# Weight conversion in a fused top-k attention and two-layer MoE kernel: first-layer conversions ordered first, the low bits formed on GpSimd, one joining step on VectorE, no zero matmuls

## The chip, the cores and the metric

The kernel runs on one core of a Trainium2 chip. The metric is the device time of one execution in microseconds (us), as the median of several runs. Five engines work in it, each with a queue that it works through in order: TensorE (PE; PEld are its weight loads), VectorE (DVE), ScalarE (ACT), GpSimd (POOL) and SyncE (SP), which here issues all DMAs.

## What is computed

Attention over 4 batches of 8 heads, 576 tokens and head dimension 64, in which each query keeps only its 32 largest scores; then two pairs of dense layers over all 2304 tokens.

```python
scores = scale * np.matmul(q, k.transpose(0, 1, 3, 2))
kth = np.partition(scores, -top_k, axis=-1)[..., -top_k:-top_k + 1]      # top_k = 32
scores = np.where(scores >= kth, scores, -1000000000.0)
scores = scores - np.max(scores, axis=-1, keepdims=True)
attn = np.exp(scores)
attn = attn / (np.sum(attn, axis=-1, keepdims=True) + 1e-09)
x = np.matmul(attn, v)          # to (2304, 512)
h = np.maximum(x @ w_in, 0.0)                                   # 512 -> 2048
x = h * h @ w_out                                               # 2048 -> 512
h = np.maximum(np.maximum(x @ w1, x @ w2), x @ w3)              # 512 -> 768
out = h @ w_out2                                                # 768 -> 512
```

[...]

## The kernel before

**Attention.** The tokens are cut into 20 tiles of 128 (or, for the last 64 tokens of a batch, 64) queries. `attend` takes a tile, for each of 4 pairs of heads: the scores of a head go from PE (L414) through ScalarE (L440) to a row of 576 per query. VectorE finds the 32 largest by four MAX (L446, eight values each) with three MATCH_REPLACE (L448) between them: seven instructions a head, 144 heads. ScalarE and GpSimd then form the exponentials and their fp16 halves (L452 to L461), SP transposes them by DMA (L462), PE multiplies by v (L470), and at the tile's end the result goes to `xt` in two fp16 halves (L505). A tile's place in the order has a rank, the number of tiles before it.

**Dense layers.** Two or three tiles make one of nine blocks. `moe1` multiplies a block by `w_in` (matmuls b<-xt,wt), applies the ReLU with a scale `u1` and squares, and accumulates the product with `w_out` in two PSUM tiles (matmuls a<-hh,wo and a<-hl,wo). Before the accumulation it writes a matmul by an all-zero tile over each of the two (L656), 18 in all. `moe2` does the second pair of layers (matmuls b<-yt,wu). All is done in fp16 halves, three matmuls to a product.

**Conversion of weights.** `convert` turns the float64 weights into scaled fp16 halves, in 28 chunks of 128 x 1024, each in two half chunks: 56 half chunks. A half chunk is loaded into a buffer `wu` of 512 pairs of words (L524; five such buffers, which later loads share). ScalarE rescales the upper word (L526, shown as L301). VectorE shifts the upper word left by 3 (L527) and the lower one right by 29 (L529), and GpSimd adds the two into a float32 chunk `w` (L531). PE forms a Gram matrix of the chunk (L538) from which a scale follows by a chain through VectorE, PE (L544) and GpSimd (L551 to L556); with it ScalarE writes the upper fp16 half (L565), and PE (L572, L573) and ScalarE (L575) the lower. `w_in`, `w1`, `w2` and `w3` go back to DRAM (`wsc`) and are loaded again for each block; `w_out` and `w_out2` stay in SBUF. Sixteen chunks belong to the first layers (eight groups of two: four "in", four "wo"), twelve to the second. After each layer's last group, `scales` reduces all scales to `u1` or `u2` (the reductions zm, L588).

**The order.** `Plan` takes every operation with an estimated duration, a priority and a rank, and lays out each engine's queue in advance: at each step, among the operations that could start within 100 ns of the best, the one with the lowest rank goes first. Nothing is reordered afterwards: an instruction that has to wait holds everything behind it on its engine. `feed` hands out the conversion steps with their ranks; the first 33 are the first layers' and their scales.

Of the kernel before, what the change touches and what calls it, by code (L numbers as in the profile page):

```python
# [68 lines left out]
class Op:  # L69
    __slots__ = ("eng", "ns", "fn", "prio", "deps", "outs", "bufs", "idx", "lat", "end", "ndep", "opens", "start", "soft", "slack", "rank")  # L70


class Plan:
# [68 lines left out]
    def run(self):  # L142
# [24 lines left out]
        while len(issued) < len(self.ops):  # L167
            best = None
            for e in engines:
                cand = []  # L170
                for o, r in pool[e]:
                    t = r
                    used = {}
                    for b in o.opens:
# [63 lines left out]
def c_pool(n):  # L238
    return 100.0 + 2.18 * n
# [11 lines left out]
def kernel(ctx, tc, q, k, v, wsrc, out, DM, FF, F2):  # L251
# [33 lines left out]
    def dve(prio, n, reads, writes, fn, rate=1.0, slack=0.0):  # L285
        return plan.op(DVE, c_dve(n, rate), prio, reads, writes, fn, slack=slack)
# [35 lines left out]
    zero = const.tile([P, P], F16, name="zero")  # L322
    nc.gpsimd.memset(zero[:], 0.0)
# [31 lines left out]
    def prep_k(b, p):  # L355
# [8 lines left out]
        gps(A_X, 2 * S, [ks, kt], [kt], lambda: sub(  # L364
# [8 lines left out]
    def prep_v(vst):  # L373
# [4 lines left out]
        pe(A_V, 107.0, [sm], [ps, sc], lambda: nc.tensor.matmul(ps[:, 0:1], ones_t[:], sm[:], start=True, stop=True))  # L378
# [38 lines left out]
    def attend(b, t, g):  # L417
# [5 lines left out]
        for p in range(NP):  # L423
# [8 lines left out]
            for h in range(1 if rem else 2):  # L432
# [60 lines left out]
        gps(A_X, DM / 2, [xg, va], [xg], lambda: nc.gpsimd.tensor_scalar(  # L493
# [16 lines left out]
    def convert(chunks, val, x, kind):  # L510
# [4 lines left out]
        for j, n in enumerate(chunks):  # L515
            for y in range(2):
                raw = buf("wu", [P, 512, 2])
                if y == 0:
# [20 lines left out]
                pe(M_, 4 * 80.0, [(w, y)], [ps, turns], gram)  # L539
# [4 lines left out]
        pe(M_, 260.0, [dg], [ps2, t0], lambda: nc.tensor.matmul(ps2[:, 0:P], up_t[:], dg[:], start=True, stop=True))  # L544
# [6 lines left out]
        gps(C_P, 50, [t0], [(val, x)], lambda: nc.gpsimd.tensor_scalar(  # L551
            vx(), t0[:], 2.0 ** (119 if root else 111), None, op0=ALU.mult))
        if root:
            gps(C_P, 50, [(val, x)], [sc], lambda: nc.gpsimd.tensor_tensor(sc[:], vx(), vx(), op=ALU.mult))
# [1 line left out]
        gps(C_P, P / 2, [sk], [di], lambda: nc.gpsimd.tensor_scalar(di[:], ident, sv(), None, op0=ALU.mult))  # L556
# [24 lines left out]
    def scales():  # L581


        def unify(a, b, f, cu, u, m):
            t = lambda: zt[:, 0:f]
            gps(C_P, 50, [a, b], [zt], lambda: nc.gpsimd.tensor_tensor(t(), a[:], b[:], op=ALU.mult))
# [9 lines left out]
        gps(C_P, 50, [zu], [r0], lambda: nc.gpsimd.tensor_tensor(r0[:], zu[:, 0:1], zu[:, 0:1], op=ALU.mult))  # L596
        gps(C_P, 50, [zu, r0], [r0], lambda: nc.gpsimd.tensor_tensor(r0[:], r0[:], zu[:, 1:2], op=ALU.mult))
# [252 lines left out]
```

## Time and profile before

| what | value |
|---|---|
| three runs | 1069.63, 1071.26 (median), 1074.93 us |
| profiled execution | 1077.44 us, its span 1075.5 us |
| PE busy | 1006.3 us (94%), 8426 matmuls |
| DVE busy | 855.7 us (80%) |
| ACT busy | 827.9 us (77%) |
| POOL busy | 658.6 us (61%) |
| chain that ended last, by engine | PE 51%, DVE 23%, DMA 8%, ACT 8%, POOL 4%, issue 4% |
| conversion loads wu<-in_w_dram | 56 of 512 KB |

The profile is one execution of the program. Busy is the time in which an engine had an instruction under way, so overlapping instructions of one engine count once; a duration is from an instruction's start to its end, and consecutive ones can overlap. The chain is followed back from the last instruction, at each step to what released it, or to the one before it on its engine.

### The profile page before, as it was taken

How to read it: one execution, taken by the hardware profiler on the slowest of the kernel's cores; microseconds unless marked ns; L12 is line 12 of the kernel's file. 1: busy time of each engine (PE TensorE's matmuls, PEld its weight loads, DVE VectorE, ACT ScalarE, POOL GpSimd, SP SyncE). 2: the span in 40 equal slices, each digit the busy share in tenths (PEclk: the TensorE clock that was granted, in tenths of full speed). 3: DMA queues.
4: the chain of work that ended last, by engine and by line, in shares of the span. 5: the costliest groups of instructions: out<-in, count | busy, mean ns of one | idle time of the engine just before them, and what ended most of it. 6: DMA issues, size and time to landing. Idle time of an engine off the chain costs nothing.

```text
span 1075.5 us, 23814 instructions
## 1 busy us (share of the span) xinstructions
PE 1006.3 (94%) x8426; PEld 797.6 (74%) x8426; DVE 855.7 (80%) x1961; ACT 827.9 (77%) x1900; POOL 658.6 (61%) x1127
## 2 busy tenths in 40 slices
PE   5768778999999999999999999999999999999998
PEld 3433334767677788798889879886987899797876
DVE  6999999999955999999999999798999994002011
ACT  6767787998998698899899879977997895351431
POOL 2676666788776566787777658865776665121111
PEclk9998877999999999999999999999999999999999
DMA  7577877998789667887976868795778657335211
GB/s 216 109 214 203 215 191 203 235 246 205 237 228 265 177 149 195 214 182 192 238 142 159 193 167 190 160 219 123 152 165 214 139 142 210 103 99 186 69 40 60
DMA packets 220535, 189.45 MB, mean 176 GB/s; under 512 B 176384, under 2 KB 185344, under 8 KB 220416
## 3 DMA queue, kind: packets, MB, share of 16 engines
q1 hardware_dynamic: 220416, 187.93, 68.8%
q8 instruction: 66, 1.08, 0.4%
q14 instruction: 53, 0.43, 0.1%
HBM read 131.79 MB, written 13.63 MB: 135 GB/s over the span
## 4 chain that ended last, share of the span: by engine, by line
PE 51%; DVE 23%; DMA 8%; ACT 8%; POOL 4%; issue 4%; SPq 1%; POOLq 0%; ACTq 0%; DVEq 0%
PE b L638 28%; PE a L638 12%; DVE mx L446 10%; DVE w L448 8%; PE b L414 4%; PE b L470 3%; DMA wu<-in_w_dram 3%; DMA et<-e 3%; PE b L572 2%; DVE wu L529 2%; DVE wu L527 1%; DVE m L722 1%; DMA vst<-in_v_dram 1%; POOL e L298 1%; ACT e L454 1%
## 5 line engine op out<-in xcount | busy, mean ns | idle before, releaser
L446 DVE MAX8 mx<-w 128x8 f32<-128x576 f32 x432 | 312.3, 746 | 0.6
L298 POOL TENSOR_TENSOR e<-e,e 128x512 f16<-128x512 f32 (+1 forms) x288 | 209.4, 739 | 73.0 <-ACT e L457 66.8
L638 PE MATMUL b<-yt,wu 128*128 128x256 f16 x1944 | 226.8, 274 | 2.2 <-ACT yt L701 0.9
L638 PE MATMUL a<-hh,wo 128*128 128x256 f16 x1152 | 221.6, 273 | 0.0
L638 PE MATMUL b<-xt,wt 128*128 128x256 f16 x1728 | 220.1, 274 | 0.7 <-DMA wt<-wsc 0.7
L448 DVE MATCH_REPLACE8 w<-mx,w 128x576 f32<-128x576 f32 x288 | 213.0, 741 | 0.0
L638 PEld LDWEIGHTS <-wu 128*128 128x128 f16 x1944 | 187.0, 99 | 27.2 <-issue 2.5
L638 PEld LDWEIGHTS <-wt 128*128 128x128 f16 x1728 | 166.5, 99 | 23.0 <-issue 1.7
L638 PEld LDWEIGHTS <-wo 128*128 128x128 f16 x1728 | 164.4, 98 | 25.3 <-issue 1.9
L414 PE MATMUL b<-kt,qt 128*128 128x288 f32 (+1 forms) x640 | 156.5, 374 | 10.7 <-DMA qt<-in_q_dram 5.1
L298 POOL TENSOR_TENSOR hl<-r,hh 128x256 f16<-128x256 f32 x144 | 97.3, 679 | 104.4 <-ACT hh L675 96.1
L638 PE MATMUL a<-hl,wo 128*128 128x256 f16 x576 | 157.0, 272 | 0.0
L414 PEld LDWEIGHTS b<-kt,qt 128*128 128x128 f32 (+1 forms) x640 | 104.4, 203 | 37.3 <-issue 14.7
L301 ACT ACTIVATE e<-s,mx 128x576 f32<-128x576 f32 x144 | 111.7, 778 | 20.9 <-DVE mx L446 19.4
L446 DVE MAX8 mx<-s 128x8 f32<-128x576 f32 x144 | 107.1, 745 | 18.6 <-ACT s L440 18.6
L454 ACT ACTIVATE e<-e,nb 128x576 f32<-128x576 f32 x144 | 112.0, 780 | 5.6 <-POOL nb L450 3.7
L440 ACT ACTIVATE s<-b 128x288 f32<-128x288 f32 x288 | 109.1, 410 | 9.3 <-PE b L414 8.6
L448 DVE MATCH_REPLACE8 w<-mx,s 128x576 f32<-128x576 f32 x144 | 106.7, 741 | 0.0
L470 PEld LDWEIGHTS <-et 128*128 128x128 f16 (+1 forms) x1440 | 84.2, 103 | 28.8 <-DMA et<-e 15.9
L672 ACT ACTIVATE r<-b,u 128x256 f32<-128x256 f32 x144 | 67.9, 476 | 47.5 <-PE b L638 46.7
L470 PE MATMUL b<-vt,et 128*128 128x129 f16 (+3 forms) x1440 | 93.0, 213 | 8.2 <-DMA et<-e 6.6
L457 ACT CAST e<-e 128x576 f16<-128x576 f32 x144 | 97.1, 676 | 0.4
(111 smaller groups left out, 1398.6 us busy)
## 6 DMA issues: line engine op xcount, KB each, us to landing
wu<-wsc SPq DMA_DIRECT2D x81, 512.0 KB, 3.9
wt<-wsc SPq DMA_DIRECT2D x72, 512.0 KB, 3.9
wu<-in_w_dram SPq DMA_DIRECT2D x56, 512.0 KB, 5.2
wsc<-oc SPq DMA_DIRECT2D x17, 512.0 KB, 4.3
ks<-in_k_dram SPq DMA_DIRECT2D x12, 576.0 KB, 4.3
qs<-in_q_dram SPq DMA_DIRECT2D x48, 128.0 KB, 3.5
vst<-in_v_dram SPq DMA_DIRECT2D x16, 320.0 KB, 3.9
out_dram<-ot SPq DMA_DIRECT2D x16, 256.0 KB, 2.4
```

Of the source, the lines that this page charges most:

```text
L298: eng.tensor_tensor(out_ap, a, b, op=ALU.subtract)
L301: return nc.scalar.activation(out_ap, src, AF.Prelu, alpha=slope, **kw)
L414: nc.tensor.matmul(ps[:, 0:HS], a, c, start=m == 0, stop=m == len(seq) - 1)
L440: act(A_S, HS, [ps], [(s, f)], lambda s=s, cs=cs, ps=ps: nc.scalar.activation(s[:, cs], ps[:, 0:HS], AF.Copy, scale=escale))
L446: dve(A_X, S, [src], [(mx, r)], lambda src=src, mx=mx, m8=m8: nc.vector.max(out=mx[:, m8], in_=src[:]))
L448: dve(A_X, S + 50, [src, (mx, r)], [w_], lambda src=src, mx=mx, m8=m8, w_=w_: nc.vector.match_replace(out=w_[:], in_to_replace=mx[:, m8], ...
L454: act(A_E, S, [e, nb], [e], lambda nb=nb, e=e: nc.scalar.activation(e[:], e[:], AF.Exp, bias=nb[:], scale=-1.0 / KEEP), psum=False, ptr=1)
L457: act(A_E, S, [e], [(e16, 0)], lambda e=e, e16=e16: nc.scalar.copy(e16[:, S:2 * S], e[:]), psum=False)
L470: nc.tensor.matmul(ps[0:n, 0:wv], et[:, mm_, c0:c1], vt[:, hh, vc, 0:wv], start=x == 0, stop=x == 8)
L529: dve(C_D, 512, [lk], [lk], lambda lo=lo: nc.vector.tensor_scalar(lo(), lo(), 29, None, op0=SHR), rate=0.5, slack=SL / 2)
L638: nc.tensor.matmul(o, x, y, start=first and i == 0 and m == 0, stop=last and i == n - 1 and m == 2)
L672: act(MA, N, [ps, u1], [r], lambda r=r, ps=ps, c=c: nc.scalar.activation(r[:, 0:N], ps[:, 0:N], AF.Relu, scale=u1[:, c // 2:c // 2 + 1]), ...
```

## The change

- A half chunk's conversion: VectorE's two shifts and GpSimd's add go. GpSimd instead forms the low three bits from the top byte of the lower word (times 1/32, less 15.5/32, rounded to an integer), and VectorE joins: upper word shifted left by 3, or the low bits, in one instruction with two SBUF inputs.
- The first 33 conversion steps get ranks from -1.97 to -1.01, below the first tile's 0 (they had 0.5); the later ones 1.56 and up in steps of 0.06 (they had 0.53 and up in steps of 0.03).
- The zero matmuls go; the first product into a PSUM tile starts the accumulation.
- In the planner the joining step waits for GpSimd's running instruction and holds GpSimd's next one, and many estimated durations are set anew.

```diff
+U8 = mybir.dt.uint8
...
+                        if e == POOL:
+                            t = max(t, held)
+                        elif o.lock:
+                            t = max(t, clock[POOL] + 20.0)
...
+            if o.lock:
+                held = t + ns
...
-    return 100.0 + 2.18 * n
+    return 110.0 + 2.0 * n
...
-                dve(C_D, 512, [hk], [hk], lambda hi=hi: nc.vector.tensor_scalar(
-                    hi().bitcast(U32), hi().bitcast(U32), 3, None, op0=SHL), rate=0.5, slack=SL / 2)
-                dve(C_D, 512, [lk], [lk], lambda lo=lo: nc.vector.tensor_scalar(
-                    lo(), lo(), 29, None, op0=SHR), rate=0.5, slack=SL / 2)
-                gps(C_P, 512, [hk, lk], [(w, y)], lambda w=w, cs=cs, hi=hi, lo=lo: nc.gpsimd.tensor_tensor(
-                    w[:, cs].bitcast(U32), hi().bitcast(U32), lo(), op=ALU.add))
+                top = lambda raw=raw: raw[:].rearrange("p n u -> p (n u)").bitcast(U8).rearrange("p (n u) -> p n u", u=8)[:, :, 3]
+                gps(C_P, 300, [lk], [lk], lambda lo=lo, top=top: nc.gpsimd.tensor_scalar(
+                    lo(), top(), 1.0 / 32.0, -15.5 / 32.0, op0=ALU.mult, op1=ALU.add))
+                dve(C_D, 512, [hk, lk], [(w, y)], lambda w=w, cs=cs, hi=hi, lo=lo: nc.vector.scalar_tensor_tensor(
+                    w[:, cs].bitcast(U32), hi().bitcast(U32), 3, lo(), op0=SHL, op1=OR), slack=SL / 2, lock=True)
...
-    C0, C1 = 0.5, 0.03
+    C0, C1 = 1.5, 0.06
...
-            rank, plan.rank = plan.rank, 0.5 + 0.0 * state['n'] if state["n"] <= 33 else C0 + C1 * (state["n"] - 33)
+            rank, plan.rank = plan.rank, -2.0 + 0.03 * state['n'] if state["n"] <= 33 else C0 + C1 * (state["n"] - 33)
...
-                if f == 0 and d % 2 == 0:
-                    pe(M_, 217.0, [hh], [(pair[d // 2], 0), (pair[d // 2], 1)], lambda d=d: nc.tensor.matmul(
-                        pair[d // 2][:].rearrange("p a n -> p (a n)"), zero[:], nid[:].unsqueeze(1).to_broadcast([P, 4, P]), start=True, stop=False))
-                also = [(pair[d // 2], 0)] if f == 2 * NA - 1 and d % 2 else []
+                also = [(pair[d // 2], 0)] if f in (0, 2 * NA - 1) and d % 2 else []
...
-                    first=False, last=f == 2 * NA - 1 and d % 2 == 1)
+                    first=f == 0 and d % 2 == 0, last=f == 2 * NA - 1 and d % 2 == 1)
```

The queue of SP at the program's start, in which kt, qt and vst are the first heads' k, q and v, and wu a half chunk of weights. Before:

```order
L351 DMA kt_126<-in_k_dram 64x1152
L351 DMA qt_134<-in_q_dram 64x256
L351 DMA vst_136<-in_v_dram 128x640
L351 DMA kt_138<-in_k_dram 64x1152
L351 DMA qt_140<-in_q_dram 64x256
L351 DMA kt_142<-in_k_dram 64x1152
L351 DMA kt_147<-in_k_dram 64x1152
L524 DMA wu_153<-in_w_dram 128x1024
```

Now, from the fourth DMA on (the three ahead of it are wu as well):

```order
L531 DMA wu_136<-in_w_dram 128x1024
L531 DMA wu_138<-in_w_dram 128x1024
L358 DMA kt_140<-in_k_dram 64x1152
L358 DMA qt_144<-in_q_dram 64x256
L358 DMA vst_146<-in_v_dram 128x640
L358 DMA kt_150<-in_k_dram 64x1152
L358 DMA qt_154<-in_q_dram 64x256
L531 DMA wu_158<-in_w_dram 128x1024
```

Five weight loads have moved ahead of the first head's inputs; before they stood behind seven of these.

The queue of VectorE at the start. Before:

```order
L321 TENSOR_SCALAR nid<-ident 128x128
L446 MAX mx_164<-s_145 128x8
L448 MATCH_REPLACE w_171<-mx_164,s_145 128x576
L446 MAX mx_164<-w_171 128x8
L446 MAX mx_188<-s_159 128x8
```

Now, in which the SCALAR_TENSOR_TENSOR are the joins:

```order
L330 TENSOR_SCALAR nid<-ident 128x128
L537 SCALAR_TENSOR_TENSOR wt_152<-wu_124 128x512
L537 SCALAR_TENSOR_TENSOR wt_152<-wu_132 128x512
L537 SCALAR_TENSOR_TENSOR wt_176<-wu_134 128x512
L537 SCALAR_TENSOR_TENSOR wt_176<-wu_136 128x512
L537 SCALAR_TENSOR_TENSOR wt_194<-wu_138 128x512
L453 MAX mx_211<-s_192 128x8
L455 MATCH_REPLACE w_217<-mx_211,s_192 128x576
```

Five joins have come ahead of the first head; before, the first shift stood behind most of eight heads.

The queue of VectorE about the first reduction of scales, zm<-zt, before:

```order
L304 TENSOR_SCALAR t_1734<-t_1734 128x1
L448 MATCH_REPLACE w_1738<-mx_1696,w_1738 128x576
L529 TENSOR_SCALAR wu_1698<-wu_1698 128x512
L527 TENSOR_SCALAR wu_1698<-wu_1698 128x512
L588 TENSOR_REDUCE zm<-zt 128x1
L589 RECIPROCAL u_90<-zt 128x4
L529 TENSOR_SCALAR wu_1712<-wu_1712 128x512
```

And now:

```order
L313 TENSOR_SCALAR ia_1561<-ss_1532 128x1
L537 SCALAR_TENSOR_TENSOR wu_1574<-wu_1473 128x512
L455 MATCH_REPLACE w_1475<-mx_1447,w_1475 128x576
L453 MAX mx_1514<-w_1530 128x8
L593 TENSOR_REDUCE zm<-zt 128x1
L594 RECIPROCAL u_88<-zt 128x4
L453 MAX mx_1447<-w_1475 128x8
```

The reduction has moved ahead of attention: 77 MAX, 58 MATCH_REPLACE and 35 joins stand before it now, 94 MAX, 71 MATCH_REPLACE and 68 shifts before; for the second reduction (not shown) 178, 134 and 56 now, 176, 132 and 112 before.

## Rows read from the trace of the kernel before

**Rows 1.** Stretches: busy us (instructions) by engine, granted clock, DMA share, GB/s
```profile
core 0: us, PE busy (x) PEld busy (x) DVE busy (x) ACT busy (x) POOL busy (x), PEclk, DMA share, GB/s
0.00:193.00 193.00, 142.87 (x630) 79.52 (x631) 174.67 (x405) 145.72 (x280) 116.50 (x191) 0.89 0.73 194
193.00:306.00 113.00, 106.45 (x867) 79.14 (x866) 112.74 (x250) 103.72 (x232) 88.28 (x134) 1.00 0.86 227
306.00:322.00 16.00, 15.40 (x143) 12.51 (x143) 3.90 (x18) 15.35 (x34) 12.79 (x23) 1.00 0.82 238
350.00:700.00 350.00, 347.87 (x3272) 296.21 (x3272) 339.53 (x775) 307.70 (x745) 256.30 (x447) 1.00 0.76 182
```

**Rows 2.** The chain of waits: start us, us, what
```profile
29.14 1.46 DVE w L448 x2
30.60 1.98 DVE mx L446 x3
...
151.54 2.07 PE b L572 x2
...
315.62 6.40 DMA wu<-wsc
...
325.52 0.86 PE b L572 x2
```

**Rows 3.** PE's timeline at the first zero matmul
```profile
196.19 0.38 PE L656 MATMUL a<-nid,zero 128*128 128x512 f16 x1
196.41 0.27 PE L638 MATMUL a<-hh,wo 128*128 128x256 f16 x1
```

**Rows 4.** The shifts: groups (busy us, mean ns), range in ns, two instructions of a timeline
```profile
L529 DVE TENSOR_SCALAR wu<-wu 128x512 uint32<-128x512 uint32 x56 | 37.6, 671 | 3.1 <-DMA wu<-in_w_dram 2.7 <-POOL vout L551 0.2 <-PE b L573 0.2
L527 DVE TENSOR_SCALAR wu<-wu 128x512 uint32<-128x512 uint32 x56 | 31.0, 555 | 1.4 <-ACT wu L301 1.3
...
L529 DVE TENSOR_SCALAR wu<-wu x56: 405/443/2214, 48.3 to 314.4; 128x512 uint32<-128x512 uint32 x56
...
211.13 2.64 POOL L298 TENSOR_TENSOR kt<-ks,kt 64x1152 fp32r<-64x1152 f32 x1 [0.31 <-POOL nb L450]
...
211.84 2.21 DVE L529 TENSOR_SCALAR wu<-wu 128x512 uint32<-128x512 uint32 x1
```

**Rows 5.** VectorE's timeline: start us, us, engine, line, operation, tiles [idle before]
```profile
8.37 0.76 DVE L446 MAX8 mx<-s 128x8 f32<-128x576 f32 x1 [6.20 <-ACT s L440]
...
153.27 0.68 DVE L298 TENSOR_TENSOR xt<-b,xt 128x512 f16<-128x512 f32 x1
153.87 0.75 DVE L446 MAX8 mx<-w 128x8 f32<-128x576 f32 x1
...
170.25 0.15 DVE L588 TENSOR_REDUCE zm<-zt 128x1 f32<-128x4 f32 x1
...
320.95 0.16 DVE L588 TENSOR_REDUCE zm<-zt 128x1 f32<-128x3 f32 x1 [0.62 <-POOL zt L586]
```

**Rows 6.** Groups of GpSimd: busy us, mean ns of one | idle before, releasers
```profile
L531 POOL TENSOR_TENSOR wt<-wu 128x512 uint32<-128x512 uint32 x32 | 34.0, 1079 | 11.6 <-PE b L572 6.8 <-ACT wu L301 2.9 <-DVE wu L527 1.8
L493 POOL TENSOR_SCALAR xg<-xg,va 128x512 f32<-128x512 f32 x16 | 11.2, 703 | 6.0 <-ACT r L672 2.5 <-ACT s L440 1.6 <-DVE ia L304 1.3
L556 POOL TENSOR_SCALAR di<-ident,v 128x128 f32<-128x128 f32 x6 | 3.8, 629 | 2.5 <-PE b L572 2.2
```

**Rows 7.** The start: stretches of 5 us, and PE's first matmuls
```profile
0.00:5.00 5.00, 0.00 (x0) 0.00 (x0) 0.84 (x1) 1.49 (x2) 1.49 (x14) 1.00 0.52 132
5.00:10.00 5.00, 4.95 (x11) 3.46 (x12) 1.58 (x3) 2.22 (x6) 0.00 (x0) 1.00 1.03 227
10.00:15.00 5.00, 3.58 (x9) 2.15 (x7) 3.96 (x9) 3.26 (x8) 0.00 (x0) 1.00 0.99 361
...
5.05 5.62 PE L414 MATMUL b<-kt,qt 64*128 64x288 f32 x11 [5.05 <-DMA qt<-in_q_dram]
```

**Rows 8.** Waits: engine, line, waited for: us in total, times, longest
```profile
PEld L538 <- POOL wt L531: 15.0, 13, 3.1
```

More of the change, by code (lines that the diff above doesn't have):

```diff
@@ L69 @@
 class Op:
-    __slots__ = ("eng", "ns", "fn", "prio", "deps", "outs", "bufs", "idx", "lat", "end", "ndep", "opens", "start", "soft", "slack", "rank")
+    __slots__ = ("eng", "ns", "fn", "prio", "deps", "outs", "bufs", "idx", "lat", "end", "ndep", "opens", "start", "soft", "slack", "rank", "lock")
 class Plan:
@@ L90, in op @@
         o.slack = slack
+        o.lock = False
         o.rank = 99.0 if eng == PE and self.rank < 0 else self.rank
@@ L151, in run @@
         cols = {}
+        held = 0.0
         pool = {e: [] for e in engines}
@@ L283, in act, with dve @@
         plan.op(ACT, c_act(n, psum, ptr), prio, reads, writes, fn)
-    def dve(prio, n, reads, writes, fn, rate=1.0, slack=0.0):
-        return plan.op(DVE, c_dve(n, rate), prio, reads, writes, fn, slack=slack)
+    def dve(prio, n, reads, writes, fn, rate=1.0, slack=0.0, lock=False):
+        plan.op(DVE, c_dve(n, rate), prio, reads, writes, fn, slack=slack).lock = lock
     def gps(prio, n, reads, writes, fn):
@@ L321 @@
     nc.vector.tensor_scalar(nid[:], ident, -1.0, None, op0=ALU.mult)
-    zero = const.tile([P, P], F16, name="zero")
-    nc.gpsimd.memset(zero[:], 0.0)
     down_t = const.tile([P, P], F32, name="down")
@@ L363, in prep_k @@
         act(A_X, 2 * S, [ks], [kt], lambda: nc.scalar.copy(flat(slice(0, P)), ks[:]), psum=False)
-        gps(A_X, 2 * S, [ks, kt], [kt], lambda: sub(
+        gps(A_X, 1308, [ks, kt], [kt], lambda: sub(
             nc.gpsimd, flat(slice(D, P)), ks[D:P], flat(slice(D, P)).bitcast(F32)))
@@ L377, in prep_v @@
         ps = buf("b", [P, 512])
-        pe(A_V, 107.0, [sm], [ps, sc], lambda: nc.tensor.matmul(ps[:, 0:1], ones_t[:], sm[:], start=True, stop=True))
+        pe(A_V, 200.0, [sm], [ps, sc], lambda: nc.tensor.matmul(ps[:, 0:1], ones_t[:], sm[:], start=True, stop=True))
         act(A_V, 1, [ps], [sc], lambda: nc.scalar.activation(sc[:], ps[:, 0:1], AF.Copy, bias=2.0 ** -100))
@@ L492, in attend @@
         ia[b, t] = ir
-        gps(A_X, DM / 2, [xg, va], [xg], lambda: nc.gpsimd.tensor_scalar(
+        gps(A_X, 277, [xg, va], [xg], lambda: nc.gpsimd.tensor_scalar(
             flat(), flat(), va[0:n], 2.0 ** 77, op0=ALU.mult, op1=ALU.mult))
@@ L538, in gram @@
                         nc.tensor.matmul(ps[:, 0:P], a, a, start=j == 0 and c == 0, stop=j == len(chunks) - 1 and c == 7)
-                pe(M_, 4 * 80.0, [(w, y)], [ps, turns], gram)
+                pe(M_, 4 * 58.0, [(w, y)], [ps, turns], gram)
             yield
@@ L543, in convert @@
         ps2 = buf("b", [P, 512])
-        pe(M_, 260.0, [dg], [ps2, t0], lambda: nc.tensor.matmul(ps2[:, 0:P], up_t[:], dg[:], start=True, stop=True))
+        pe(M_, 290.0, [dg], [ps2, t0], lambda: nc.tensor.matmul(ps2[:, 0:P], up_t[:], dg[:], start=True, stop=True))
         dve(C_D, P, [ps2], [t0], lambda: nc.vector.tensor_reduce(t0[:], ps2[:, 0:P], op=ALU.max, axis=mybir.AxisListType.X))
@@ L550, in convert @@
         dve(C_D, 1, [t0], [t0], lambda: bits(t0[:], t0[:], 2 if root else 1, EXP, SHR, AND))
[L551 removed]
+        gps(C_P, 75, [t0], [(val, x)], lambda: nc.gpsimd.tensor_scalar(
             vx(), t0[:], 2.0 ** (119 if root else 111), None, op0=ALU.mult))
         if root:
[L554 removed]
+            gps(C_P, 75, [(val, x)], [sc], lambda: nc.gpsimd.tensor_tensor(sc[:], vx(), vx(), op=ALU.mult))
         sv, sk = (lambda: sc[:], sc) if root else (vx, (val, x))
[L556 removed]
+        gps(C_P, 243, [sk], [di], lambda: nc.gpsimd.tensor_scalar(di[:], ident, sv(), None, op0=ALU.mult))
         for j, n in enumerate(chunks):
@@ L585, in unify @@
             t = lambda: zt[:, 0:f]
-            gps(C_P, 50, [a, b], [zt], lambda: nc.gpsimd.tensor_tensor(t(), a[:], b[:], op=ALU.mult))
+            gps(C_P, 75, [a, b], [zt], lambda: nc.gpsimd.tensor_tensor(t(), a[:], b[:], op=ALU.mult))
             zx = lambda: zm[:, m:m + 1]
@@ L595, in scales @@
         dve(C_D, 2, [(zm, 0), (zm, 1)], [zu], lambda: nc.vector.reciprocal(zu[:, 0:2], zm[:]))
-        gps(C_P, 50, [zu], [r0], lambda: nc.gpsimd.tensor_tensor(r0[:], zu[:, 0:1], zu[:, 0:1], op=ALU.mult))
-        gps(C_P, 50, [zu, r0], [r0], lambda: nc.gpsimd.tensor_tensor(r0[:], r0[:], zu[:, 1:2], op=ALU.mult))
+        gps(C_P, 75, [zu], [r0], lambda: nc.gpsimd.tensor_tensor(r0[:], zu[:, 0:1], zu[:, 0:1], op=ALU.mult))
+        gps(C_P, 75, [zu, r0], [r0], lambda: nc.gpsimd.tensor_tensor(r0[:], r0[:], zu[:, 1:2], op=ALU.mult))
         yield
@@ L690, in total @@
                 nc.tensor.matmul(ps[:, 0:1], down_t[:], yq[:, d:d + 1], start=d == 0, stop=d == KD - 1)
-        pe(A_S, 107.0 * KD, [yq], [ps, ga], total)
+        pe(A_S, 812.0, [yq], [ps, ga], total)
         dve(A_S, 1, [ps], [ga], lambda: bits(ga[:], ps[:, 0:1], EXP, EXP, AND, XOR))
@@ L695, in moe1 @@
             gx[:].bitcast(U32), ga[:].bitcast(U32), EXP, None, op0=XOR))
-        gps(C_P, 50, [gx, r0], [gx], lambda: nc.gpsimd.tensor_scalar(
+        gps(C_P, 75, [gx, r0], [gx], lambda: nc.gpsimd.tensor_scalar(
             gx[:], gx[:], r0[:], 2.0 ** 29, op0=ALU.mult, op1=ALU.mult))
@@ L702, in moe1 @@
                 yv(0), av(d), AF.Copy, scale=ga[:]), ptr=1)
-            dve(A_S, N, [pair[d // 2], ga, (y, d)], [(y, d)], lambda d=d, yv=yv: nc.vector.scalar_tensor_tensor(
+            dve(A_S, 1.18 * N, [pair[d // 2], ga, (y, d)], [(y, d)], lambda d=d, yv=yv: nc.vector.scalar_tensor_tensor(
                 yv(1), av(d), ga[:], yv(0), op0=ALU.mult, op1=ALU.subtract), slack=SL / 4)
```

20 lines of the change are left out of this document (10 added, 10 removed).

## The prediction

> **What bounds the kernel now.** I read the busy time by stretch first, then the chain of waits, then single instructions of VectorE (DVE). [rows 1] has three regimes. Up to 193 us TensorE (PE) is busy 142.9 of 193 us, at a mean granted clock of 0.89, so part of the time at the 1.2 GHz level: two L572 matmuls in the chain took 2.07 us at 151 us and 0.86 us at 325 us [rows 2]. DVE is busy 174.7 of 193, and the chain passes between DVE, weight loads and PE. From 193 to 306 us DVE has no gap (112.7 of 113) and PE loses 6.5 us. From 306 to 322 us DVE is busy 3.9 of 16: the last conversions go round by ACT, PE and a reload of converted weights (315.62 to 322.02, [rows 2]), and then the second layer of the first block starts. After that PE is the bound: 347.9 of 350 us between 350 and 700, while DVE, busy 339.5, has little to spare. So a microsecond that brings the first 322 us to the same state earlier comes off the end; a microsecond saved on DVE alone after that does not, but one off PE does.
>
> **The sum's own time.** Durations are from an execution of 1077.4 us (span 1075.5 and 1.9 around it). The median shown is 1071.3, 0.6% below it. I work out a difference and take it off the median.
>
> **Zero products.** A zero matmul holds PE until the next starts, 0.22 us (196.19 to 196.41, [rows 3]; its 0.38 us overlaps the next). There are 18, 14 of them after PE has become the bound: 14 x 0.22 = 3.1 us. The 4 earlier ones lie in the stretch that DVE bounds and count nothing; if DVE were not the bound there, they are worth 0.9 more.
>
> **One join for two shifts.** Before, each of 56 half chunks cost DVE L529 and L527, mean 671 and 555 ns [rows 4]. Consecutive DVE instructions overlap by 0.08 (153.27, 0.68 long, the next at 153.87, [rows 5]), so the pair costs 0.671 + 0.555 - 0.16 = 1.07 us. Unhindered one is 0.41; the rest, 0.41 a pair, is waiting: at 211.84 a shift lasted 2.21 us, and ended as GpSimd's 2.64 us instruction of 211.13 did [rows 4]. The join does not occur before. Nearest is the two-input L298 of 128x512 at 153.27, 0.60 us to the next. With one wait of the average, 0.20, a join is 0.80. Bounds: 0.60 without waits, 1.07 if it waits as long as the pair. I take 0.80, since one instruction stands where two could be held. Saving 0.27 x 56 = 15 us, between 0 and 26.
>
> The row shows a single-source shift of 512 in 0.41, a two-input instruction in 0.68. The Trainium skill (VectorE: DVE Perf Modes, The perf-mode tier table) says a one-source fp32 instruction in SBUF streams two elements a cycle and a two-input one a single element, so joining two shifts saves no streaming; the rows agree (2 x 0.33 against 0.60), and by that alone the saving would be 0.07 x 56, about 4 us. It also says (SBUF — State Buffer, Who interferes with whom) that an instruction with two SBUF inputs still excludes a GpSimd one that reads SBUF; no row here has that form, and without it the join would be the 0.60 of the lower bound.
>
> **GpSimd.** It loses an add of 1.08 us and gains a byte step per half chunk [rows 6]. One-input rows: 703 ns for 512 elements (L493), 629 for 128 (L556). I take 0.70, by the equal element count: 0.38 x 56 = 21 us less on GpSimd. If L556's rate held, four times 629, 2.5 us, it would be 80 us more. GpSimd has the room for the first (116.5 of 193 busy), not comfortably for the second. ScalarE's instruction per half chunk stays.
>
> **The order: start.** SP now issues five 512 KB weight loads before the first kt. Until 15 us the queues moved 132 x 5, 227 x 5 and 361 x 5 kB = 3.6 MB [rows 7]; the five loads plus kt, qt and vst are 3.3 MB, landing near 14.2. From PE's start at 5.05, on qt's landing, to the first MAX at 8.37 were 3.3 us [rows 5, 7], so the first MAX comes at 17.5, 9.1 late; five joins (4.0) are done meanwhile. Net loss 5.1 us of DVE.
>
> **To the first layer's scales.** They free the first block's ReLU. Before, the reduction stood behind 94 MAX, 71 MATCH_REPLACE and 68 shifts, at 170.25 us [rows 5]. Now it stands behind 77, 58 and 35 joins. At 0.66 and 0.73 each (1.98 for three, 1.46 for two, [rows 2]): 17 x 0.66 + 13 x 0.73 = 20.7; 34 x 1.07 - 35 x 0.80 = 8.4; less 5.1: 24.0 us earlier by DVE's work. The chain there is half made of loads and slow matmuls that this does not shorten; the eight conversions have a longer stretch, but less attention fills the gaps between them. I take 18, giving 152 us; with nothing left of the order's gain it is 170.
>
> **To the last scales and the second layer.** The attention put off falls due here. Between the two reductions DVE has 101 MAX for 82, 76 MATCH_REPLACE for 61, 21 joins for 44 shifts: 12.5 + 11.0 - (23.5 - 16.8) = 16.8 us more. Before, the stretch was 320.95 - 170.25 = 150.7, with DVE free for 12.1 of 306 to 322; that room takes the first 12.1, and 4.7 remain. So the second reduction comes 18 - 4.7 = 13.3 us earlier, near 308. PE has the same work behind it there, so the end follows. What is late next is DVE, whose 12 us of room is used up; attention behind it has the room of PE's bound stretch.
>
> Sum: 13.3 + 3.1 = 16.4, say 16 us. 1071.3 - 16 = **1055 us**.
>
> **Rivals.** (1) *More comes through*: joins find GpSimd idle and cost 0.60. Then 56 x 0.20 = 11 us more, and up to 6 from the first scales: 1038 to 1047. For it: GpSimd is used less. Against: its queue is busy 88 of 113 us where shifts waited longest. (2) *The join waits as the pair did*: 56 x 0.27 = 15 us of the gain goes, 1070, no measurable change. For it: the 2.21 us shift; a wait can come from one long instruction. (3) *Slower: DVE is held at its queue's head by GpSimd.* Before, GpSimd's add was the last step and only PE waited for it (15.0 us in 13 waits of L538 for wt, 1.15 each, [rows 8]). Now its step stands before DVE's, and attention behind a join cannot pass it in DVE's queue. At 0.28 us of such waiting per join the 16 us are gone; at 0.60, half PE's wait, 56 x 0.60 = 34 us is lost, and the end is 1071 - 16 + 34 = 1089. For it: GpSimd does its own queue in order, conversions stand early, and the byte form is unpriced. Against: the byte step needs only the load, not ScalarE, so it can run ahead. (4) *The early conversions only move the load*: the first scales come no earlier, and 4.7 us of what is due later is not covered: 1071 - 3 + 5, about 1073. I count it with (2).
>
> **How the numbers follow.** Forecast (1047 to 1063) 0.50, rival 1 0.19, rivals 2 and 4 0.17, rival 3 0.14. A difference of 0.5%, 5.4 us, is about what a measurement tells from none; that is 1066 to 1077. Rival 1 and the forecast are faster, and a little of rival 2 (0.03): faster 0.72, same 0.14, slower 0.14. The range goes from rival 1's end, 1039, to 1074, past rivals 2 and 4; rival 3 and a tail are left out.
>
> **What would show it.** First MAX near 17 us. Joins with a mean duration near 0.88 (0.80 and the overlap): 0.68 says rival 1, 1.1 and more rival 2. The first zm reduction near 152, the second near 308, and matmuls of yt and wu right after; DVE still full between. GpSimd's byte step near 0.70; 2.5 would bring rival 3, which the waits of DVE's joins for GpSimd show. No zero matmul. PE full after 310. It is wrong if the first reduction is not earlier than 165, or if PE's later stretch grows gaps that the 2 us of 350 to 700 did not have.

## The result and the profile after

| | before | after |
|---|---|---|
| median | 1072.58 us (4 runs, 1069.63 to 1074.93) | 1060.38 us (4 runs, 1055.52 to 1062.58) |
| ratio | | 0.9881, 95% interval 0.9838 to 0.9925 |
| profiled execution | 1077.44 us (span 1075.5) | 1062.58 us (span 1060.8) |
| chain by engine | PE 51, DVE 23, DMA 8, ACT 8% | PE 64, DMA 12, ACT 9, DVE 9% |

The kernel became 12.7 us faster by the ratio (8.0 to 17.4); the forecast was 16. Line numbers have moved: MAX is L453, the join L537, the byte step L535, the reductions zm L593, the slow conversion matmuls L577.

Stretches of the kernel after, to hold against [rows 1] (same columns):

```profile
0.00:193.00 193.00, 149.27 (x682) 82.77 (x683) 156.72 (x355) 146.64 (x283) 103.75 (x188) 0.82 0.78 209
193.00:306.00 113.00, 106.37 (x875) 81.18 (x873) 103.62 (x238) 104.25 (x234) 85.44 (x140) 0.98 0.79 211
306.00:322.00 16.00, 14.83 (x118) 10.60 (x117) 13.27 (x34) 15.22 (x34) 12.45 (x28) 1.00 0.98 279
350.00:700.00 350.00, 348.51 (x3309) 298.92 (x3307) 341.03 (x777) 308.32 (x743) 253.49 (x447) 1.00 0.74 182
```

VectorE is no longer full from 193 to 306 us (103.6 of 113, 112.7 before), and up to 193 us it is busy 18 us less. TensorE is 6.4 us busier there, but at a lower granted clock (0.82, before 0.89). The room of 306 to 322 is mostly used up, as forecast (13.3 us busy of 16).

The first MAX and the two reductions on VectorE's timeline of the kernel after, which answer to [rows 5]:

```profile
15.95 0.76 DVE L453 MAX8 mx<-s 128x8 f32<-128x576 f32 x1 [3.60 <-ACT s L447]
...
156.59 0.14 DVE L593 TENSOR_REDUCE zm<-zt 128x1 f32<-128x4 f32 x1
...
316.13 0.14 DVE L593 TENSOR_REDUCE zm<-zt 128x1 f32<-128x3 f32 x1
```

The first is 13.7 us earlier than before, the second only 4.8.

Groups of the kernel after (busy us, mean ns of one | idle time before them, releasers): the join, and GpSimd's byte step. They answer to [rows 4, 6].

```profile
L537 DVE SCALAR_TENSOR_TENSOR wt<-wu 128x512 uint32<-128x512 uint32 x32 | 21.7, 703 | 11.5 <-POOL wu L535 7.7 <-PE b L577 3.7
L537 DVE SCALAR_TENSOR_TENSOR wu<-wu 128x512 uint32<-128x512 uint32 x24 | 17.3, 728 | 0.1
...
L535 POOL TENSOR_SCALAR wu<-wu 128x512 uint32<-128x512 uint8 x56 | 36.9, 659 | 41.5 <-DMA wu<-in_w_dram 30.2 <-DVE mx L453 6.9 <-PE b L421 1.6
```

A join lasts 0.71 us on the mean of all 56, hardly more than the 0.68 of the two-input instruction of [rows 5], so it almost never waits once it has begun. The byte step, 0.66, mostly waits for its load.

The chain of the kernel after between 80 and 130 us (start us, us, what; compare [rows 2]):

```profile
85.77 2.44 DMA qt<-in_q_dram
88.28 1.65 POOL di L561
89.97 2.07 PE b L577 x2
...
102.99 4.01 DMA wu<-in_w_dram
107.01 5.95 DMA et<-e
...
119.60 6.93 DMA et<-e
```

It goes round by loads, transposes and matmuls at 2.07 us a pair, with VectorE a small part.

How busy each engine was up to the first reduction, and from it to the second, before:

```profile
0.00:170.25 170.25, 122.98 (x536) 68.65 (x536) 154.18 (x359) 126.73 (x245) 102.77 (x168) 0.91 0.72 189
170.25:320.95 150.70, 141.10 (x1099) 102.20 (x1100) 136.78 (x309) 137.04 (x298) 114.13 (x178) 0.95 0.85 228
```

and after:

```profile
0.00:156.59 156.59, 115.07 (x494) 62.80 (x495) 123.67 (x281) 115.71 (x222) 82.09 (x151) 0.81 0.77 207
156.59:316.13 159.54, 150.39 (x1143) 108.59 (x1144) 146.70 (x337) 145.32 (x318) 115.65 (x192) 0.96 0.81 216
```

Up to the first reduction VectorE has 30.5 us less work (154.2 to 123.7), but the reduction is only 13.7 us earlier: VectorE now idles 32.9 us instead of 16.1. Between the two it has 9.9 us more work, as the attention that was put off falls due.

Where the 14.7 us between the two spans went shows in TensorE's matmuls by time. The kernel before, to 400 us and after it:

```profile
0.00:400.00 400.00, 342.20 (x2320) 233.37 (x2321) 354.87 (x816) 327.75 (x690) 266.12 (x437) 0.94 0.78 207
400.00:1000.00 600.00, 594.51 (x5532) 506.68 (x5530) 492.87 (x1127) 473.69 (x1148) 378.92 (x669) 1.00 0.70 171
```

The kernel after:

```profile
0.00:400.00 400.00, 347.99 (x2375) 237.86 (x2376) 336.69 (x771) 331.02 (x706) 250.81 (x444) 0.91 0.79 209
400.00:1000.00 600.00, 596.94 (x5592) 510.90 (x5590) 489.50 (x1116) 477.54 (x1148) 378.23 (x667) 1.00 0.69 172
```

From 400 us on TensorE is almost full in both, at 600 / 5592 = 0.107 us a matmul. By 400 us the kernel after has done 55 matmuls more (5.9 us), and between 400 and 1000 another 60 (6.4 us). So only some 6 of the 15 us come from the stretch on which the whole forecast stood.

The other 60 can't be put down to the change. The profiled execution of before took 1077.44 us, while all its other runs, those beside the experiments included, took 1067.35 to 1075.11. Most of the 60 are missing between 700 and 800 us, where a load of v took 7.00 us (from the chain: start us, us, what) and TensorE did 907 matmuls (stretch, columns as in [rows 1]):

```profile
724.24 7.00 DMA vst<-in_v_dram
700.00:800.00 100.00, 96.64 (x907) 82.06 (x906) 92.75 (x213) 84.90 (x214) 66.06 (x122) 0.98 0.73 159
```

In that stretch the kernel after did 946. Two kernels of the experiments that are nearly the kernel before, with the zero matmuls out (1.) and with one estimate moved by 1 ns (7.), did 949 and 951, and from 400 to 1000 us:

```profile
400.00:1000.00 600.00, 596.49 (x5595) 511.98 (x5593) 488.63 (x1118) 475.08 (x1150) 379.71 (x669) 1.00 0.69 172
400.00:1000.00 600.00, 598.76 (x5610) 513.03 (x5609) 489.41 (x1121) 476.21 (x1152) 380.26 (x669) 1.00 0.68 172
```

Against these two the kernel after is some 33 matmuls ahead by 400 us (2341 and 2342, for 2375), and not ahead later.

### The profile page after: what moved, and what is told of

It reads as the page before. It is cut to its first block, busy times and chain, and to the rows that moved or that the text cites. A ratio compares the mean times of both kernels' runs of the same rounds, so it can differ in the third digit from the quotient of the medians.

```text
span 1060.8 us, 23745 instructions
## 1 busy us (share of the span) xinstructions
PE 999.8 (94%) x8408; PEld 793.1 (75%) x8408; DVE 834.1 (79%) x1905; ACT 827.7 (78%) x1900; POOL 638.8 (60%) x1126
## 4 chain that ended last, share of the span: by engine, by line
PE 64%; DMA 12%; ACT 9%; DVE 9%; POOL 3%; issue 3%; SPq 0%; POOLq 0%; ACTq 0%; DVEq 0%
PE b L643 32%; PE a L643 14%; PE b L421 8%; DMA et<-e 6%; PE b L477 5%; DVE mx L453 3%; DVE w L455 3%; PE b L577 3%; DMA wu<-in_w_dram 3%; DMA qt<-in_q_dram 2%; ACT e L461 1%; ACT e L310 1%; ACT junk L686 1%; POOL e L307 1%; ACT e L464 1%
## 5 line engine op out<-in xcount | busy, mean ns | idle before, releaser
L453 DVE MAX8 mx<-w 128x8 f32<-128x576 f32 x432 | 313.6, 751 | 0.6
L643 PE MATMUL a<-hh,wo 128*128 128x256 f16 x1152 | 218.4, 273 | 0.0
L643 PEld LDWEIGHTS <-wt 128*128 128x128 f16 x1728 | 164.2, 98 | 24.6 <-issue 2.8
L310 ACT ACTIVATE e<-s,mx 128x576 f32<-128x576 f32 x144 | 112.2, 780 | 13.4 <-DVE mx L453 11.0
L453 DVE MAX8 mx<-s 128x8 f32<-128x576 f32 x144 | 107.9, 750 | 10.9 <-ACT s L447 10.9
```

The lines of the kernel that those rows point to most:

```text
L310: return nc.scalar.activation(out_ap, src, AF.Prelu, alpha=slope, **kw)
L453: dve(A_X, S, [src], [(mx, r)], lambda src=src, mx=mx, m8=m8: nc.vector.max(out=mx[:, m8], in_=src[:]))
L643: nc.tensor.matmul(o, x, y, start=first and i == 0 and m == 0, stop=last and i == n - 1 and m == 2)
```

## The experiments

Theories: **A**, the forecast's: VectorE's work ahead of the two reductions sets the time. **B**: it isn't VectorE any more, and other bounds early on (loads, TensorE at the lower clock) or the planner's order decide. Differences in us are the ratio's distance from 1 times 1071.3.

**1. The zero products alone.** The kernel before with these lines only:

```diff
-                if f == 0 and d % 2 == 0:
-                    pe(M_, 217.0, [hh], [(pair[d // 2], 0), (pair[d // 2], 1)], lambda d=d: nc.tensor.matmul(
...
-                    first=False, last=f == 2 * NA - 1 and d % 2 == 1)
+                    first=f == 0 and d % 2 == 0, last=f == 2 * NA - 1 and d % 2 == 1)
```

> The kernel before with only the 18 zero products left out (nothing of the output is lost). If the spacing of 0.22 us that was read in the trace is what TensorE is late by in each block, the time falls by 9 x 2 x 0.19 to 0.22 = 3.4 to 4.0 us, to about 1068.5 to 1069 where before has 1072.5, and the second zm stays where it was (near 321 in the profile) because VectorE sets it. If half of the products lay in time that TensorE waits anyway, it falls by under 2 us.

Ratio 0.9992 (0.9971 to 1.0013): 0.9 us less, at most 3.1. The same from the other side, the zero products put back into the kernel after (the diff above, reversed):

> The kernel after with the 18 zero products put back. If each costs TensorE 0.19 to 0.22 us in a stretch that it bounds, 3.4 to 4 us more than after (1063.5 to 1064.5 beside 1060.4); under 2 us if they fit into waits.

Ratio 0.9884 (0.9866 to 0.9903), where the kernel after has 0.9881: no difference, though the interval of after (0.9838 to 0.9925) is too wide to tell 3 us from none. The trace of that kernel shows that TensorE is held as forecast:

```profile
427.18 0.38 PE L663 MATMUL a<-nid,zero 128*128 128x512 f16 x1
427.39 0.27 PE L645 MATMUL a<-hh,wo 128*128 128x256 f16 x1
```

0.21 us to the next matmul. But with 18 operations more the planner found another order: by 400 us this kernel had 2468 matmuls done, the kernel after 2375; from 400 to 1000 us it did 5550, the kernel after 5592. So the local price holds, and the total doesn't show it.

**2. The new conversion alone.** The kernel before with the byte step, the join and the planner's rule for it; old ranks, old estimates, zero products in:

```diff
-                dve(C_D, 512, [hk], [hk], lambda hi=hi: nc.vector.tensor_scalar(
...
+                dve(C_D, 512, [hk, lk], [(w, y)], lambda w=w, cs=cs, hi=hi, lo=lo: nc.vector.scalar_tensor_tensor(
+                    w[:, cs].bitcast(U32), hi().bitcast(U32), 3, lo(), op0=SHL, op1=OR), slack=SL / 2, lock=True)
```

> The kernel before with the new conversion alone (GpSimd's byte step, VectorE's join, the planner's rule that keeps GpSimd free during a join), with the zero products, the old ranks of the conversions and the old estimates. Theory A, the forecast's: VectorE's 56 x (1.23 - 0.70) = 30 us less work ahead of the second zm comes through, second zm 10 to 20 us earlier than 320.95, time 8 to 15 us less (1057 to 1064). Theory B, VectorE's saved time is eaten by other bounds (loads, TensorE at half clock, ScalarE) in the first 320 us: second zm 0 to 6 us earlier, time 3 to 7 us less (1065 to 1069). Both: mean of a join 0.68 to 0.75 us.

Ratio 0.9904 (0.9881 to 0.9928), 10.3 us less: A by the time. But the reductions were at 168.12 and 337.68 us, the second 17 us *later* than before. A's mechanism fails where its number holds.

**3. The new ranks alone**, with the two shifts and the add:

```diff
-    C0, C1 = 0.5, 0.03
+    C0, C1 = 1.5, 0.06
...
+            rank, plan.rank = plan.rank, -2.0 + 0.03 * state['n'] if state["n"] <= 33 else C0 + C1 * (state["n"] - 33)
```

> The kernel before with the conversions' new ranks alone (first layers ahead of the first tile's attention, second layers later), old conversion with two shifts and GpSimd's add, zero products in. If the early conversions only move VectorE's load (a rival of the prediction), first zm comes 5 to 12 us earlier, second zm within 3 us of 320.95, time within 3 us of 1072.5. If VectorE, now full to the second zm, is held more by GpSimd's adds at the start, it is 3 to 8 us slower.

Ratio 0.9921 (0.9897 to 0.9945), 8.5 us less; reductions at 136.63 and 293.46. Neither expectation holds: the early conversions don't only move the load.

The ranks also do something that the diff doesn't show, by a line that is the same in both kernels:

```python
        o.rank = 99.0 if eng == PE and self.rank < 0 else self.rank
```

A TensorE operation with a rank below 0 gets 99. So the new ranks put the first layers' conversions first on the other four queues, and their matmuls last among those that TensorE could start at about the same time. No run takes the two apart.

**4. The new estimates alone.** No instruction differs, only durations by which the planner orders:

```diff
-    return 100.0 + 2.18 * n
+    return 110.0 + 2.0 * n
...
-                pe(M_, 4 * 80.0, [(w, y)], [ps, turns], gram)
+                pe(M_, 4 * 58.0, [(w, y)], [ps, turns], gram)
```

> The kernel before with only the planner's new estimates of durations (24 of them, mostly GpSimd's and two of VectorE's and TensorE's); no instruction is added or taken away, only their order differs. If the 5 to 7 us that the kernel after gains between 320 us and its end beyond the zero products come from a better order by these estimates, this kernel takes 1066 to 1069; if they come from the conversion being over earlier or from VectorE's room, it takes 1071 to 1074.

Ratio 0.9875 (0.9850 to 0.9901), 13.4 us less: as much as the whole change. The kernel after with the old estimates:

> The kernel after with the old 24 estimates of durations in the planner, all else as after. If the estimates carry the later part of the gain: 4 to 7 us more than after (1064 to 1067). If they carry nothing: within 1.5 us of after (1059 to 1062).

Ratio 0.9829 (0.9812 to 0.9846), 5.6 us *faster* than after, though the two intervals still touch. Both are outside what either expectation had; the same numbers are worth 13 us in one setting and seem to cost 6 in another.

**5. The old ranks in the kernel after** (the diff of 3, reversed):

> The kernel after with the old ranks of the conversions (first layers at the rank of the tile after the first, second layers from 0.5 on). Theory A, VectorE's work ahead of the two zm's sets the time: first zm later by 10 to 18 us (near 170), second zm earlier or the same, time within 3 us of after. Theory B, the first blocks' TensorE start sets it: 3 to 8 us slower than after (1063 to 1068). If the early loads of weights at the start cost more than they give (first MAX 15.95 instead of 8.37), it is 2 to 5 us faster than after.

Ratio 0.9916 (0.9902 to 0.9929), 3.7 us slower than after; that is B's side, but the two intervals overlap. The first reduction is at 168 us, as A had it; the second, which A had earlier or the same, is 32 us later than after. VectorE's timeline of this kernel, the end of the second block's first layers (`ga`) and the second reduction:

```profile
334.04 0.16 DVE L313 TENSOR_SCALAR ga<-b 128x1 uint32<-128x1 uint32 x1 [0.96 <-PE b L692]
...
347.94 0.14 DVE L593 TENSOR_REDUCE zm<-zt 128x1 f32<-128x3 f32 x1
```

The second reduction is 27 us later than before, and the kernel 9 us faster than before. TensorE doesn't stand still for it: it did the second block's first layers meanwhile.

**6. Without the rule for the joins.** The same instructions as after, in another order:

```diff
-                    w[:, cs].bitcast(U32), hi().bitcast(U32), 3, lo(), op0=SHL, op1=OR), slack=SL / 2, lock=True)
+                    w[:, cs].bitcast(U32), hi().bitcast(U32), 3, lo(), op0=SHL, op1=OR), slack=SL / 2)
```

> The kernel after without the planner's rule that puts a join only where GpSimd is free (in the plan) and holds GpSimd for its length; the instructions are the same, their order differs. If that rule is why a join takes 0.70 us and not the 0.80 that was forecast, the joins' mean rises to 0.80 or more, GpSimd's mean in its other steps rises, and the time is 1 to 4 us more. If joins rarely meet GpSimd anyway, mean 0.68 to 0.72 and the time within 1 us of after.

Ratio 0.9757 (0.9738 to 0.9777), median 1046.58 us, the fastest of all: 13 us less than after, where 1 to 4 more were expected. Its joins do wait, as expected:

```profile
L537 DVE SCALAR_TENSOR_TENSOR wt<-wu 128x512 uint32<-128x512 uint32 x32 | 24.0, 774 | 9.8 <-POOL wu L535 6.4 <-PE b L577 1.8 <-POOL nb L457 1.0
L537 DVE SCALAR_TENSOR_TENSOR wu<-wu 128x512 uint32<-128x512 uint32 x24 | 23.9, 997 | 0.5 <-issue 0.3 <-POOL wu L535 0.2
```

Mean of the 56: 0.87 us, 8.9 us in all more than after; GpSimd's byte step rose from 0.66 to 0.71. The longest join on VectorE's and GpSimd's timelines:

```profile
265.45 3.02 DVE L537 SCALAR_TENSOR_TENSOR wu<-wu 128x512 uint32<-128x512 uint32 x1
268.39 0.08 DVE L455 MATCH_VALUE_LOAD w<-mx,w 128x8 f32 x1
```

```profile
265.30 2.62 POOL L307 TENSOR_TENSOR kt<-ks,kt 64x1152 fp32r<-64x1152 f32 x1
268.00 1.63 POOL L307 TENSOR_TENSOR hl<-r,hh 128x256 f16<-128x256 f32 x2
```

The join of 265.45 lasted until GpSimd's instruction had ended at 267.92, and 0.55 more. Yet the reductions came at 129.03 and 274.66. Stretches up to the first, and between them:

```profile
0.00:129.03 129.03, 94.31 (x448) 53.77 (x449) 111.36 (x249) 104.47 (x201) 80.19 (x139) 0.88 0.85 235
129.03:274.66 145.63, 134.39 (x969) 94.13 (x967) 139.68 (x308) 132.16 (x280) 102.64 (x167) 0.93 0.83 223
```

Up to the second reduction VectorE is busy 251.0 us and idle 23.6; after, 270.4 and 45.8. The queue goes with the smaller busy time: with the rule 77 and 178 MAX stand before the two reductions, without it 66 and 156. In the planner's code a join under the rule can't start until GpSimd's running instruction ends; where that is more than 100 ns away, attention is placed first, whatever the rank.

**7. The rule in three more settings, and a shake.** The new conversion alone (2), the kernel after with old estimates (4) and with old ranks (5), each without the rule, by the edit of 6:

> The kernel before with the new conversion alone (as e2_conv_only: old ranks, old estimates, zero products in), and the rule that keeps GpSimd free during a join left out. Theory A, the rule costs more than the waits that it spares: joins' mean 0.80 to 1.0 us (0.70 in e2_conv_only), both zm reductions at least 10 us earlier than in e2_conv_only (168, 338), time 5 to 15 us less than its 1060.5. Theory B, the 14 us that e7_no_lock gained on the kernel after are chance of the order: within 5 us of 1060.5, either side.

Ratio 0.9857 (0.9838 to 0.9875), 5.0 us less than with the rule; joins 0.79, reductions 6 and 38 us earlier. That is A's side, with the first reduction less early than it asked.

> The kernel after without the rule for the joins and with the old estimates. The old estimates gave 5 us with the rule (e8_old_costs 1055.4); the new ones gave 13 us without a join (e4_costs_only). If the rule alone costs, this kernel takes 1040 to 1047; if the old estimates' 5 us came from weakening the rule (GpSimd is held for other lengths), 1047 to 1055.

Ratio 0.9858 (0.9836 to 0.9879), median 1056.04: slower by 3.1 us than with the rule (the two intervals overlap), outside both expectations.

> The kernel after without the rule for the joins and with the old ranks. If the early conversions are worth what the forecast had for the order's part (first zm 18 us earlier, some 5 us of the time), this kernel is 3 to 10 us slower than e7_no_lock (1049 to 1057) and its first zm comes near 160 instead of 129. If the joins' freedom does it all, it is within 3 us of e7_no_lock.

Ratio 0.9867 (0.9842 to 0.9892), 11.8 us slower than 6 and 5.2 faster than 5; first reduction at 170, not 160. In these two pairs the new ranks do more where the rule is off.

And the kernel before with one estimate moved by 1 ns:

```diff
-    return 100.0 + 2.18 * n
+    return 101.0 + 2.18 * n
```

> The kernel before with one estimate of the planner moved by 1 ns (GpSimd's fixed part, 101 for 100): no instruction changes, and no reason speaks for a gain or a loss; only the order that the planner finds differs here and there. It measures how much an arbitrary other order is worth. If orders of this planner differ little, within 2 us of before; if parts of 5 to 10 us can come from a different order alone (as the 13 us of e4_costs_only, and the zero products that are worth nothing in e1_zeros_out and e5_zeros_back, would suggest), 4 to 12 us to either side.

Ratio 0.9957 (0.9942 to 0.9972), 4.6 us less: the second expectation.

All kernels, by setting (MAX ahead of the two reductions are counted in VectorE's queue; matmuls and zm are from the profiled execution):

| kernel | ratio (95%) | us | MAX ahead of zm | zm at, us | join ns | matmuls by 400 us | profiled us |
|---|---|---|---|---|---|---|---|
| before | 1 | 0 | 94, 176 | 170, 321 | – | 2320 | 1077.4 |
| before, shaken | 0.9957 (0.9942–0.9972) | −4.6 | 94, 176 | 169, 319 | – | 2342 | 1066.5 |
| before, zeros out | 0.9992 (0.9971–1.0013) | −0.9 | 94, 176 | 166, 321 | – | 2341 | 1066.4 |
| before, new ranks | 0.9921 (0.9897–0.9945) | −8.5 | 65, 163 | 137, 293 | – | 2422 | 1060.0 |
| before, new estimates | 0.9875 (0.9850–0.9901) | −13.4 | 96, 176 | 164, 311 | – | 2462 | 1055.1 |
| before, new conversion | 0.9904 (0.9881–0.9928) | −10.3 | 99, 186 | 168, 338 | 703 | 2391 | 1062.6 |
| ... without the rule | 0.9857 (0.9838–0.9875) | −15.3 | 94, 176 | 162, 299 | 791 | 2480 | 1055.8 |
| after | 0.9881 (0.9838–0.9925) | −12.7 | 77, 178 | 157, 316 | 714 | 2375 | 1062.6 |
| ... without the rule | 0.9757 (0.9738–0.9777) | −26.0 | 66, 156 | 129, 275 | 870 | 2564 | 1045.1 |
| after, zeros back | 0.9884 (0.9866–0.9903) | −12.4 | 77, 176 | 155, 320 | 732 | 2468 | 1057.7 |
| after, old ranks | 0.9916 (0.9902–0.9929) | −9.0 | 101, 190 | 168, 348 | 722 | 2373 | 1064.5 |
| ... without the rule | 0.9867 (0.9842–0.9892) | −14.2 | 91, 174 | 170, 306 | 785 | 2393 | 1062.0 |
| after, old estimates | 0.9829 (0.9812–0.9846) | −18.3 | 71, 176 | 142, 323 | 768 | 2448 | 1056.3 |
| ... without the rule | 0.9858 (0.9836–0.9879) | −15.2 | 67, 159 | 142, 288 | 800 | 2449 | 1061.0 |

Four readings.

- **The shake.** An edit with no meaning is worth 4.6 us (3.0 to 6.2). A single comparison of this kernel with a re-planned one therefore can't give one part a price below about 5 us, however narrow its interval. (It is one shake; how far others would move the time, no run shows.) The parts alone sum to 0.9 + 10.3 + 8.5 + 13.4 = 33 us, and the whole gives 12.7.
- **The rule.** In all four pairs it shortens the joins (by 32 to 156 ns each) and puts more attention ahead of the reductions (10 to 22 MAX ahead of the second). Without it the time is 13.3, 5.0 and 5.2 us less, and 3.1 us more with the old estimates: 5 us on the mean. That it sets joins and conversions so is shown. That it costs time is not: four values from -3 to 13 don't tell their mean from none, and a part of the 13 can be the luck of one order.
- **The conversion.** The nine kernels with the join lie 9.0 to 26.0 us below before (mean 14.8), the five with two shifts 0 to 13.4 (mean 5.5). The 9 us between the means are a rough estimate of what the new conversion brings, since the other parts are not spread evenly over the two sets.
- **What goes with the time** is not the second reduction (293 us: −8.5; 338: −10.3; 348: −9.0) but how many matmuls TensorE has done by 400 us: from 2373 (1064.5 us) to 2564 (1045.1) that is 0.10 us each, near the 0.107 of one matmul in the full stretch. This says where the time is won, and not by which part of the change. The stretch behind adds its own differences: in the kernel with old estimates and no rule it held 5531 matmuls from 400 to 1000 us, 5576 with the rule, and by 400 us the two were level (2449 and 2448), though its second reduction is 35 us earlier. Why that stretch came out worse there is open.

## Why the prediction was right, and where its steps failed

The time, 1060, lies 5 us from the forecast and within its own range of 1047 to 1063. Its working held in part: the sizes of single instructions did, the way from VectorE's work to the end did not, so that the number came so near is in good part luck.

**Zero products (3.1 us).** The hold of 0.21 to 0.22 us is in the trace. In the total, 0.9 us (at most 3.1) came when they were taken out, and no difference when they were put back. The term is smaller than what a new order does by chance; whether 3 us lie under that stays open.

**The join at 0.80.** It came out at rival 1's price: 0.71 mean duration, where 0.88 was to be seen. The step that failed is "with one wait of the average, 0.20": it passed over the planner's rule, which the diff has and which keeps GpSimd clear. Where that rule is off, the joins last 0.79, 0.79, 0.80 and 0.87. So 0.88 was the price, or a little over it, of a join left to itself, and with the rule the saving of 15 us was 56 x (0.88 - 0.71) = 9 us too low. Rival 1's time (1038 to 1047) didn't follow: VectorE idled more than it was spared.

The join also settles the form that no row showed before: two SBUF inputs, and excluded by GpSimd (3.02 us at 265.45). The Trainium skill (SBUF — State Buffer, Who interferes with whom) says that a VectorE instruction with two SBUF inputs contends with a GpSimd instruction that reads SBUF; the trace agrees. It also says that the order of issue decides who blocks. The last section has rows of the other direction, which agree for the first of four joins only: the other three began after GpSimd's step and still went before it.

**GpSimd.** Byte step 0.66 for 0.70; its conversion work fell from 58.9 us (the 56 adds) to 36.9, by 22 where 21 were counted. Rival 3 fell: VectorE's joins waited 7.7 us in 6 waits for it, with the loads still under way.

**Start.** First MAX 15.95, forecast 17.5; 8.76 with the old ranks. Right.

**First reduction: 18 us earlier was taken, 13.7 came.** VectorE's busy time ahead of it fell by 30.5 us, where 20.7 + 8.4 = 29.1 were counted: the 35 joins were cheaper than taken, but so were the 34 pairs of shifts that they replaced (562 and 525 ns on the mean of those, 671 and 555 of all). What was missed is how far VectorE's idle time would grow: from 16.1 to 32.9 us, by 16.8. Of that 4.3 lie before the first MAX, where the forecast had 5.1; the other 12.5 stand against the 6 that it took off. Its longest waits there are those of its diagonals for the Gram matrices, of its joins for the byte step and for buffers that PE frees, and of attention's reciprocals for GpSimd:

```profile
DVE wt L537 <- POOL wu L535: 7.7, 6, 3.8
DVE dg L547 <- PE b L543: 7.5, 5, 3.7
DVE rc L485 <- POOL rc L483: 5.6, 4, 2.3
DVE wt L537 <- PE b L577: 3.7, 2, 3.0
```

(VectorE's waits up to 173 us of the kernel after: waited for, us in total, times, longest.) "Half made of loads and slow matmuls" was in the text; the term taken off for it was half of what it came to.

**Second reduction: 13.3 us earlier was taken, 4.8 came**, and "the end follows" is the step that is wrong. In three kernels the second reduction is later than before by 2 to 27 us, and they are 9.0 to 18.3 us faster. TensorE goes on with the first layers of the next block. What the early stretch has to deliver is matmuls, from whatever layer. By 400 us some 6 us had come, against the 13.3; the 6.4 after that are not the change's, as shown above, and where the rest of the measured 12.7 us lies, the one profile of each kernel doesn't show.

**Rivals.** 2 fell (joins didn't wait). 4 fell: the ranks alone gave 8.5 us and a first reduction 34 us earlier, and 3.7 (within the noise) and 11.8 us in the two pairs of after. What no rival held is that the planner's estimates, which the forecast gave no price at all, move the time by 13 us alone: as much as the whole change. So which part of the change brought its 12.7 us stays open.

**Signs named.** DVE full between the reductions: wrong, 146.7 of 159.5. PE without gaps later: right, 348.5 of 350.

## What to carry to other kernels

Where a planner lays out every queue, first shake it: move one estimate by nothing, and see how far the time goes; edits worth less than that are priced by several settings, on the mean, and not by one comparison. Hold the profiled execution against the kernel's other runs before a difference of 1% is split over stages. A wait that a rule avoids is to be set against what the rule puts off: here it spared 9 us of VectorE's waits, and put 22 more MAX ahead of the second reduction. Look for the count of what the final bound has done by some time, not for one milestone, when that engine can take other work meanwhile.

## What the runs showed of the hardware

**One-element work on GpSimd behind joins.** Four joins in a row, with GpSimd's instruction at the same time (timelines of the kernel after):

```profile
64.18 2.49 DVE L537 SCALAR_TENSOR_TENSOR wt<-wu 128x512 uint32<-128x512 uint32 x4
```

```profile
64.36 2.40 POOL L556 TENSOR_SCALAR vin<-t 128x1 f32<-128x1 f32 x1
66.75 0.26 POOL L483 TENSOR_SCALAR rc<-xs,sc 128x2 f32<-128x2 f32 x1
```

A GpSimd step that moves one element per partition lasted 2.40 us, until all four joins were through; a like one of two elements behind them took 0.26. The other 13 such steps of that line took 0.22 to 0.66. So these four joins, one behind the other without a break, left no gap for it; it is one case, and no run was made for it.

**The clock.** Two stretches of TensorE before (columns as in [rows 1]):

```profile
0.00:50.00 50.00, 33.55 (x111) 21.71 (x112) 40.85 (x88) 36.29 (x77) 19.89 (x44) 1.00 0.61 162
50.00:100.00 50.00, 34.67 (x154) 19.15 (x153) 47.00 (x109) 32.99 (x62) 33.59 (x44) 0.90 0.74 204
```

and after:

```profile
0.00:50.00 50.00, 30.94 (x105) 18.06 (x106) 34.34 (x74) 31.97 (x59) 19.76 (x42) 0.94 0.86 246
50.00:100.00 50.00, 41.40 (x174) 21.48 (x173) 39.34 (x89) 40.83 (x84) 33.40 (x53) 0.72 0.72 196
```

After a first stretch in which TensorE did a little less than before (30.9 us, 33.6 before), the grant of the second fell to 0.72 (0.90 before), so over half of it ran at the 1.2 GHz level. That first stretch alone doesn't settle it: two other kernels, zeros back and old estimates, did 30.3 and 30.5 us in theirs, and were granted 0.67 and 0.85 in the second. Of the 6.7 us that TensorE was busier there, part is matmuls that took longer, such as the pair of 2.07 us at 89.97. No run here separates how much of the change's gain that cost.
